# Where an expert's rows are zeroed and on which queue they are loaded: moving clears, loads and one weight split in a fused attention and mixture-of-experts kernel

## The chip, the cores and the metric

The kernel runs on one core of a Trainium2 chip. The metric is device time in microseconds (us), the median of several executions. One execution is recorded by the hardware profiler; its rows are what the prediction reads. PE is the matmul engine, PEld its weight loads, DVE the vector engine, ACT the scalar engine, POOL the GpSimd engine, SP the engine that only issues DMAs (its rows carry SPq).

## The reference, cut to what matters

Three layers follow each other; the output of one is the input of the next.

```python
# 1. recurrent attention over 2 x 8 heads, 768 positions, head size 48
for t in range(S):
    cur = einsum('bhd,bhe->bhde', u * k[t], v[t])
    y[t] = einsum('bhd,bhde->bhe', r[t], state + cur)
    state = w * state + einsum('bhd,bhe->bhde', k[t], v[t])
# 2. mixture of 8 experts, 1536 tokens of 384 numbers, each token to its best expert
expert = argmax(x @ w_gate); pos = rank of the token among those of its expert
disp[expert, pos] = x                      # dropped at capacity 384
y = relu(disp @ w1) @ w2                   # w1: 384 -> 1024, w2: 1024 -> 384
out = gate * y[expert, pos]                # 0 for a dropped token
# 3. gated MLP
out = (sigmoid(x @ w_gate2) * (x @ w_val)) @ w_out      # 384 -> 1536 -> 384
```

## The kernel before

**Stages.** Attention runs in eight steps `s` (a batch and a pair of heads each). The experts run in 64 steps `i` of one loop (line 1010), `i = 8e + f` for expert `e` and eighth `f` of its hidden layer. The gated MLP follows. The order of work on every engine is written out by hand: instructions go to each engine's queue in the order of the code, and each engine works through its own queue in that order.

**Rows of an expert.** Attention's output rows are sent to a table `xs_d` in device memory, 1536 rows for each expert, with indirect DMAs on POOL (`scatter`, line 231, twelve in all, six for each batch). A block of 224 rows per expert is read back. Rows of the block that no token fills must be zero. Before, this is done in two ways. For experts 0, 1 and 2 (`ZS = 3`), zeros are written to the whole block during attention step 3 from SP (line 742), where a source block `z_d` of zeros is written too. For experts 3 to 7, `clear(e)` (line 851) copies `z_d` over the 224 rows behind the expert's last token, at a place known only at run time, from POOL, at steps 11, 12, 13, 14 and 16 (`ZE`). Since the place is known only at run time, each of these copies counts as a write to the whole table: it waits for earlier copies and earlier reads of the table, and later reads wait for it.

**Loading an expert.** `eload(e)` (line 936) brings the 224 rows into a tile `xr` (two buffers). Expert 0 comes another way (`pre`, `first`). `eload(1)` is issued on POOL at step 0, `eload(2)` on SP at step 9, and `eload(e + 2)` on SP at `f == 7` of experts 1 to 5, so `eload(3)` at step 15 and `eload(4)` at step 23. `escale(e)` (line 943) then multiplies both halves by the gate on ACT, at step 7 for expert 1 and at `f == 3` of the expert before for the others (step 11 for expert 2, step 19 for expert 3). `etr(e, b)` (line 948) transposes half `b` on PE, and ACT and DVE split the result into a high and a low part; both halves share one buffer in PSUM. For expert 1 both are at step 8, each followed by an `s2`; for the others at `f == 4` and `f == 6` of the expert before.

**One step.** `s1` (nine matmuls, line 973) makes a piece of the hidden layer, ACT and DVE split it (lines 975, 976), and `s2` (six matmuls, lines 991 and 992) of a step three before adds to the output. `bg` (line 145) splits one raw weight tile of 128 x 768 into a high part on ACT (line 154) and a low part on DVE (line 156). Step `i` splits tile `n = 4 + i`, at the end of the step, behind that step's ACT work. Five raw buffers exist; `bg` of tile `n` first asks SP for tile `n + 5` (`fetch`, line 136), whose DMA waits until the buffer of tile `n` was read. `s1` of step `i` reads the tile with the largest even number not above `i`.

**Two extra waits.** Raw tile 5 waits for the landing of expert 0's rows, and raw tile 9 (`XG = 9`) for the landing of `eload(1)` (lines 142 and 143). Tile 9 is split at step 5.

**Decode.** From step 11 on, `tick` takes one piece at a time of the decode of the MLP's weights (lines 166 to 200), with a DMA of 768 KB for each tile on SP and a subtraction on POOL.

Of the kernel before, what the change touches and what calls it, by code (L numbers as in the profile page):

```python
# [21 lines left out]
AHEAD = 5  # L22
# [8 lines left out]
WE = 1  # L31
WF = 7
WG = 5
ZS = 3
ZE = {11: 3, 12: 4, 13: 5, 14: 6, 16: 7}
XG = 9
NKR = 3
NV = 4
ND = 5
# [1 line left out]
BG = (0, 0, 0, 0, 0, 0, 4, 0)  # L41
NB = 224
NP = NB // 2
# [5 lines left out]
MT = 5  # L49
HPB = 6  # L50
OVP = 60
BG2 = (56,)
NT = 2
TAILF = 4
EB0 = 8
# [61 lines left out]
def body(tc, A, out):  # L117
    nc = tc.nc
    E = mybir.EngineType
    with ExitStack() as top, tc.manual_schedule():  # L120
# [3 lines left out]
        xs_d = dr.tile([8 * 1536 + NB, XW], F32, tag="xs_d", name="xs_d")  # L124
        z_d = dr.tile([NB, XW], F32, tag="z_d", name="z_d")
# [10 lines left out]
        def fetch(n):  # L136
            while nxt[0] < n:
                m = nxt[0]
                nxt[0] += 1
                raw[m] = rpl[0].tile([128, 768], F32, tag="raw", name="raw", bufs=rpl[1])  # L140
                i = nc.sync.dma_start(out=raw[m], in_=A["wx"][m // 2][:, (m % 2) * 768:(m % 2) * 768 + 768])
                if m in (sum(BG) + 1, XG):
                    after(i, xr1l if m == XG else xr0l)

        def bg(count=1, pool=False, ahead=3, later=None, cast=nc.scalar.copy):
            for _ in range(count):
# [78 lines left out]
                    if k == 4:  # L225
                        last = n

        scx, sci, sco, xr0l, xr1l = [], [], [], [], []

        def scatter(done, group, dst, index, src, rows):  # L230
            i = nc.gpsimd.indirect_dma_start(  # L231
# [7 lines left out]
        def after(load, done):  # L239
            for i in done:  # L240
                tc.add_manual_dep(load.ins, i.name,
                                  mybir.DependencyInfo(mybir.DependencyClass.Sync, mybir.DependencyReason.DATA),
                                  reason="rows of every scatter")
# [22 lines left out]
        with ExitStack() as ctx:  # L266
# [17 lines left out]
            zero = cp.tile([128, 2, XW], F32, tag="zero", name="zero")  # L284
# [371 lines left out]
            def consts():  # L656
# [5 lines left out]
                nc.gpsimd.iota(tid, pattern=[[128, 12]], base=0, channel_multiplier=1)  # L662
                nc.gpsimd.tensor_copy(out=capf, in_=capi)

            def ok(q):
                return 0 <= q < 8

# [20 lines left out]
            for i in range(2):  # L688
# [7 lines left out]
                           in_=w128.unsqueeze(2).unsqueeze(2).to_broadcast([112, 4, 48, 4]))  # L696
# [34 lines left out]
            for s in range(8):  # L731
                nx, fu = s < 7, s < 6
                if s < 4:
                    load(s + 4, "k")
                if s < 5:
                    load(s + 3, "v")
                if s < 4:
                    load(s + 4, "d")
                fetch(sum(BG[:max(s + 2, 4)]) if s else 0)
                if s == 3:  # L740
                    for z in [xs_d[e * 1536:e * 1536 + NB, :] for e in range(ZS)] + [z_d]:
                        nc.sync.dma_start(out=z.rearrange("(p b) d -> p b d", b=2), in_=zero[0:NP])
                if s == 2:
                    consts()
                if nx:
                    ap0 = a_mm(s + 1, C0)
                    ap1 = a_mm(s + 1, C1)
                    u_pe(s + 1)
                subs = []
                y_own(s, C1)  # L750
                if s == 6:
                    diag(7, range(8, 12))
                out_evac(s, 1 if nx else 2)
                if nx:
                    out_tr(s)
                    a_cp(s + 1, C0, ap0)
                    u_scan(s + 1)
                    if s == 6:
                        bg(1, False, 0, subs, nc.vector.tensor_copy)
                        bg(BG[s] - 1, False, 0, subs)  # L760
                        subs.pop(0)()
                    out_x(s, s == 6)
                if s == 5:
                    r3b(0)
                    r3c(0)
                if fu:
                    rp(s + 2)
                    out_l(1)
                    sums(s + 2)
                    diag(s + 2, range(8))  # L770
                    out_l()
                    if s == 3:
                        r1a(0)
                    if s == 4:
                        r1o(0)
                    last = kb(s + 2)
                    a_cp(s + 1, C1, ap1)
                    if s < 5:
                        behind(kk_part(s + 2), last)
                        pr_part(s + 3, P_)  # L780
                    else:
                        kk_part(7, V_)
                if s == 6:
                    a_cp(7, C1, ap1)
                    for f in subs:
                        f()
                    cnt(0)
                if nx:
                    y_in(s + 1)
                    if s == 6:  # L790
                        y_own(7, (0, 1))
                        out_evac(7, 0)
                        y_own(7, (2, 3))
                        out_evac(7, 1)
                    else:
                        y_own(s + 1, C0)
                        out_evac(s + 1, 0)
                    if s < 5:
                        diag(s + 2, range(8, 12))
                    if s == 3:  # L800
                        r1m(0)
                    if s == 4:
                        r2(0)
                        r3a(0)
                        r1s(0)
            fetch(sum(BG) + 1)
            out_tr(7)
            warm_up(WF)
# [21 lines left out]
        with ExitStack() as ctx:  # L830
# [4 lines left out]
            xr, xt = {}, {}  # L835
# [15 lines left out]
            def clear(e):  # L851
                r = nc.values_load(zoi[0:1, e:e + 1], engines=[E.Pool], min_val=0, max_val=8 * 1536,
                                   skip_runtime_bounds_check_because="behind an expert's rows")
                nc.gpsimd.dma_start(out=xs_d[bass.ds(r, NB), :], in_=z_d)

            def overflow():
                with tc.If(offv["most"] > NB):  # L857
# [75 lines left out]
                offv[e] = nc.values_load(offi[0:1, e:e + 1], engines=[E.DVE, E.Activation], min_val=0, max_val=1536,  # L933
                                         skip_runtime_bounds_check_because="expert counts sum to the number of tokens")

            def eload(e, eng=nc.sync):
                xr[e] = mp.tile([128, 2, XW], F32, tag="xr", name="xr")
                i = eng.dma_start(out=xr[e][0:NP], in_=xs_d[e * 1536:e * 1536 + NB, :].rearrange("(b p) d -> p b d", p=NP))
                after(i, scx)
                if e == 1:  # L940
                    xr1l.append(i.ins)

            def escale(e):
                for b in range(2):
# [65 lines left out]
            for i in range(64 + LAG):  # L1010
                if i == OVP:
                    overflow()
                if i < 64:
                    e, f = seq[i]
                    if i == EB0:
                        for b in range(2):
                            etr(1, b)
                            s2(0, 5 + b)
                    s1(e, f)
                    if i == IC2:  # L1020
                        c2(0)
                        c2(1)
                    if i == IC1:
                        c1()
                    if i == OVL:
                        offv["most"] = nc.values_load(mxi[0:1, 0:1], min_val=0, max_val=1536,
                                                      skip_runtime_bounds_check_because="at most every token")
                    if i in ZE:
                        clear(ZE[i])
                    if f == 3 and e:  # L1030
                        c3(e)
                    if i == EB0 - 1 or f == EB[0] - 1 and 0 < e < 7:
                        escale(e + 1)
                    if f in EB and 0 < e < 7:
                        etr(e + 1, EB.index(f))
                    if f == 7 and 0 < e < 6 or i == 9:
                        eload(e + 2 if i != 9 else 2)
                if i >= LAG:
                    e, f = seq[i - LAG]
                    if i < 66 - TAILF:  # L1040
                        for g in (() if f == 0 and e else (0, 1) if f == 1 and e else S20.get(i, (f,))):
                            s2(e, g)
                        if (f == 7 if i > max(S20) else i == EB0):
                            for m in range(3):
                                yev(e, m)
                    elif i == 66:
                        for m in range(3):
                            for g in range(7 - TAILF, 8):
                                s2(7, g, (m,))
                            yev(7, m)  # L1050
                            xsplit(0, m)
                if i <= 58:
                    bg(2 if i in BG2 else 1, False, AHEAD)
                if i == 0:
                    eload(1, nc.gpsimd)
                if i == LOAD1:
                    tick()
                if i < 64:
                    tick(0 if i < T0 or OVP - NT <= i < OVP else TK if i < 51 else 2)
# [98 lines left out]
```

## Time and profile before

| | us |
|---|---|
| median of 3 executions | 457.27 |
| lowest, highest | 456.75, 458.99 |
| the profiled execution, its own time | 458.45 |
| its span, first to last instruction | 456.8 |
| PE busy in it | 435.9 (95%) |
| DVE busy | 283.4 (62%) |
| ACT busy | 226.1 (49%) |
| POOL busy | 108.4 (24%) |

Attention takes the first 76 us of the span, the experts run from 76 to 223 us, the gated MLP from 223 us to the end. Busy shares are averages over these three parts. In timelines a row is a start, a duration, an engine, a line and an operation, and in square brackets how long the engine had been idle before it and which instruction ended that. Rows of matmuls overlap in part, since matmuls are pipelined.

### The profile page before, as it was taken

What the parts mean: (1) busy time and instruction counts of PE and PEld (TensorE: products, weight loads), DVE (VectorE), ACT (ScalarE), POOL (GpSimd) and SP (SyncE); (2) the same over time, 40 slices, a digit from 0 to 9 for tenths busy, and PEclk for the clock granted to TensorE, in tenths of its full rate; (3) what the DMA queues carried; (4) which work ended last, traced back from release to release, by engine and by line L of the source; (5) the groups of instructions that cost most, each with busy time, mean ns of one, the idle gap of its engine ahead of it and who ended that gap; (6) DMA issues with size and microseconds to landing.
All of it is one profiled execution on the core that took longest, in us unless ns stands there. A gap on an engine that the chain in (4) does not pass through costs nothing.

```text
span 456.8 us, 8304 instructions
## 1 busy us (share of the span) xinstructions
PE 435.9 (95%) x3212; PEld 417.1 (91%) x3215; DVE 283.4 (62%) x498; ACT 226.1 (49%) x490; POOL 108.4 (24%) x107
## 2 busy tenths in 40 slices
PE   8999999899589999999999999999999999999993
PEld 4788888789589999999999999999999999999993
DVE  6888997559658898995577877778432221212211
ACT  5587687457357687775534353443442222222131
POOL 2466756000010110230033642322122000000013
PEclk9999999979869999999999999999999999999998
DMA  7999937558597987775025352431001000000002
GB/s 239 327 274 237 343 113 254 167 191 294 205 346 212 274 258 245 235 170 168 13 70 90 119 116 93 138 108 32 1 37 67 1 1 0 1 0 1 1 17 86
DMA packets 21946, 63.37 MB, mean 139 GB/s; under 512 B 4672, under 2 KB 6624, under 8 KB 21824
## 3 DMA queue, kind: packets, MB, share of 16 engines
q1 hardware_dynamic: 19584, 55.97, 40.9%
q0 software_dynamic: 2176, 6.84, 4.1%
q8 instruction: 26, 0.43, 0.4%
q14 instruction: 16, 0.13, 0.1%
q10 hardware_dynamic: 144, 0.00, 0.0%
HBM read 56.66 MB, written 7.88 MB: 141 GB/s over the span
## 4 chain that ended last, share of the span: by engine, by line
PE 51%; issue 1%; POOL 1%; POOLq 0%; ACT 0%
PE pg L1081 17%; PE pv L1081 16%; PE po L1106 16%; PE py L992 1%; PE ph L973 1%; POOL out_dram L231 1%; PE py L991 1%; POOLq L1154 0%; ACT sg L1087 0%; POOLq L231 0%
## 5 line engine op out<-in xcount | busy, mean ns | idle before, releaser
L1091 DVE TENSOR_TENSOR sg<-sg,pv 128x384 f32<-128x384 f32 (+2 forms) x49 | 26.6, 543 | 80.0 <-PE pv L1081 80.0
L156 DVE TENSOR_TENSOR rl<-raw,rh 128x768 fp32r<-128x768 f32 x60 | 59.9, 1000 | 20.0 <-ACT rh L154 19.6
L992 PE MATMUL py<-hh,rh 128*128 128x448 f32 x192 | 66.5, 387 | 0.0
L1092 ACT CAST gh<-sg 128x384 fp32r<-128x384 f32 (+2 forms) x49 | 24.8, 506 | 78.5 <-DVE sg L1091 78.4
L154 ACT CAST rh<-raw 128x768 fp32r<-128x768 f32 x63 | 52.2, 834 | 6.1 <-DMA raw<-in_wx_dram 5.7
L991 PE MATMUL py<-hh,rl 128*128 128x224 f32 x192 | 54.2, 282 | 0.0
L1093 DVE TENSOR_TENSOR gl<-sg,gh 128x384 fp32r<-128x384 f32 (+2 forms) x49 | 35.6, 727 | 28.9 <-ACT gh L1092 28.9
L1087 ACT ACTIVATE sg<-pg 128x384 f32<-128x384 f32 x48 | 23.6, 491 | 59.0 <-PE pg L1081 58.8
L200 POOL TENSOR_TENSOR wy<-wa,wy 128x768 fp32r<-128x768 f32 x10 | 19.7, 1968 | 107.9 <-ACT wy L196 107.9
L992 PEld LDWEIGHTS py<-hh,rh 128*128 128x128 f32 x192 | 38.0, 198 | 2.3
L975 ACT ACTIVATE hh<-ph 128x224 fp32r<-128x224 f32 x64 | 22.9, 357 | 34.8 <-PE ph L973 34.5
L231 POOL DMA_INDIRECT out_dram<-ob,ids x12 | 11.7, 974 | 118.5 <-ACT ob L1113 116.1
L991 PEld LDWEIGHTS py<-hh,rl 128*128 128x128 f32 x192 | 38.6, 201 | 0.0
L1106 PE MATMUL po<-wy,gh 128*128 128x384 f32 x144 | 36.6, 335 | 0.0
L976 DVE SCALAR_TENSOR_TENSOR hh<-ph,hh 128x224 fp32r<-128x224 f32 x64 | 24.6, 385 | 13.0 <-ACT hh L975 12.4
L419 ACT ACTIVATE at<-cst,dl 128x128 f32<-128x128 f32 x88 | 27.3, 389 | 5.8 <-DVE dl L405 4.8
L973 PE MATMUL ph<-xh,rh 128*128 128x224 f32 x96 | 26.6, 277 | 0.3 <-PEq L857 0.3
L973 PE MATMUL ph<-xl,rh 128*128 128x224 f32 x96 | 26.8, 279 | 0.0
L973 PE MATMUL ph<-xh,rl 128*128 128x224 f32 x96 | 26.7, 279 | 0.0
L973 PE MATMUL ph<-xeh,rh 128*128 128x224 f32 x96 | 26.6, 280 | 0.0
L973 PE MATMUL ph<-xel,rh 128*128 128x224 f32 x96 | 26.4, 279 | 0.0
L973 PE MATMUL ph<-xeh,rl 128*128 128x224 f32 x96 | 26.3, 278 | 0.0
(215 smaller groups left out, 1195.3 us busy)
## 6 DMA issues: line engine op xcount, KB each, us to landing
raw<-in_wx_dram SPq DMA_DIRECT2D x64, 384.0 KB, 4.8
r<-in_wy_dram SPq DMA_DIRECT2D x18, 768.0 KB, 5.5
kt<-in_kr_dram SPq DMA_DIRECT2D x7, 576.0 KB, 9.9
dm<-in_dm_dram SPq DMA_DIRECT2D x5, 672.0 KB, 12.4
v<-in_v_dram SPq DMA_DIRECT2D x8, 288.0 KB, 10.1
xr<-xs_d SPq DMA_DIRECT2D x6, 339.5 KB, 5.0
dm<-in_dm_dram SPq DMA_DIRECT2D x6, 288.0 KB, 11.8
xs_d<-z_d POOLq DMA_DIRECT2D x5, 339.5 KB, 5.5
```

The lines of the kernel that those rows point to most:

```text
L154: cast(out=h, in_=t)
L156: (nc.gpsimd if pool else nc.vector).tensor_sub(rl[n % NR], t, h.bitcast(F32))
L419: nc.scalar.mul(AT[s][:, j, :], ident, DL[s][:, j:j + 1])
L973: nc.tensor.matmul(ph, a[:, w], b[:, kt, :], start=(i == 0), stop=(i == 8))
L976: nc.vector.scalar_tensor_tensor(out=h[:, 1, :], in0=ph, scalar=0.0, in1=h[:, 0, :].bitcast(F32), op0=ALU.max, op1=ALU.subtract)
L991: nc.tensor.matmul(y[:, 0, :], wl[:, w], h[:, 0, :], start=(f == 0), stop=False, skip_group_check=True)
L992: nc.tensor.matmul(y, wh[:, w], h, start=False, stop=(f == 7), skip_group_check=True)
L1081: nc.tensor.matmul(pg[g], w[a][:, q], x[b][:, kt, :], start=(kt == 0 and (a, b) == (0, 0)), stop=(kt == 2 and b == 1))
L1091: nc.vector.tensor_mul(gg[:, a:b], sg[:, a:b], pg[1][:, a:b])
L1092: nc.scalar.copy(out=gh[:, a:b], in_=gg[:, a:b])
L1093: nc.vector.tensor_sub(gl[:, a:b], gg[:, a:b], gh[:, a:b].bitcast(F32))
L1106: nc.tensor.matmul(po[i], g[v][:, a], w[u][:, q], start=(f == 0 and (u, v) == (0, 0)), stop=(f == 11 and v == 1))
```

## The change

- `ZS` goes from 3 to 5: the blocks of experts 0 to 4 are zeroed during attention step 3, and the source block `z_d` is written at step 6 in place of step 3.
- The clears that are left, for experts 5, 6 and 7, move to steps 21, 22 and 23, and are declared independent of one another.
- `eload(1)` moves from POOL's queue to SP's, at the same step 0, which is ahead of raw tile 9 in SP's queue. Raw tile 9 no longer waits for its landing.
- `eload(e + 2)` of experts 1 to 5 moves from `f == 7` to `f == 4`: `eload(3)` from step 15 to 12, `eload(4)` from 23 to 20, `eload(5)` from 31 to 28.
- Step 5 splits no weight tile, and step 11 splits two. From step 6 to step 10, a step splits tile `3 + i`.

```diff
-ZS = 3
-ZE = {11: 3, 12: 4, 13: 5, 14: 6, 16: 7}
-XG = 9
+ZS = 5
+ZE = {21: 5, 22: 6, 23: 7}
+GE = 4
-BG2 = (56,)
+BG2 = (11, 56)
+BG0 = (5,)
...
-                if m in (sum(BG) + 1, XG):
-                    after(i, xr1l if m == XG else xr0l)
+                if m == sum(BG) + 1:
+                    after(i, xr0l)
...
+            def zfill(d):
+                nc.sync.dma_start(out=d.rearrange("(p b) d -> p b d", b=2), in_=zero[0:NP])
...
                 if s == 3:
-                    for z in [xs_d[e * 1536:e * 1536 + NB, :] for e in range(ZS)] + [z_d]:
-                        nc.sync.dma_start(out=z.rearrange("(p b) d -> p b d", b=2), in_=zero[0:NP])
+                    for e in range(ZS):
+                        zfill(xs_d[e * 1536:e * 1536 + NB, :])
+                if s == 6:
+                    zfill(z_d)
...
-                nc.gpsimd.dma_start(out=xs_d[bass.ds(r, NB), :], in_=z_d)
+                i = nc.gpsimd.dma_start(out=xs_d[bass.ds(r, NB), :], in_=z_d).ins
+                tc.declare_no_dep(i, group="zc", reason="each expert has rows of its own")
+                tc.add_to_no_dep_group("zc", i)
...
-            def eload(e, eng=nc.sync):
+            def eload(e):
                 xr[e] = mp.tile([128, 2, XW], F32, tag="xr", name="xr")
-                i = eng.dma_start(out=xr[e][0:NP], in_=xs_d[e * 1536:e * 1536 + NB, :].rearrange("(b p) d -> p b d", p=NP))
-                after(i, scx)
-                if e == 1:
-                    xr1l.append(i.ins)
+                after(nc.sync.dma_start(out=xr[e][0:NP], in_=xs_d[e * 1536:e * 1536 + NB, :].rearrange("(b p) d -> p b d", p=NP)), scx)
...
-                    if f == 7 and 0 < e < 6 or i == 9:
+                    if f == GE and 0 < e < 6 or i == 9:
                         eload(e + 2 if i != 9 else 2)
...
-                    bg(2 if i in BG2 else 1, False, AHEAD)
+                    bg(0 if i in BG0 else 2 if i in BG2 else 1, False, AHEAD)
                 if i == 0:
-                    eload(1, nc.gpsimd)
+                    eload(1)
```

## Rows read from the trace of the kernel before

**Rows 1.** The page: TensorE's granted clock, tenths, in 40 equal slices.

```profile
PEclk9999999979869999999999999999999999999998
```

**Rows 2.** Waits of PE: who waited, for whom; us in total, times, longest us.

```profile
PE xp L955 <- ACT xr L946: 8.9, 3, 6.2
...
PE ap L438 <- DVE dm L397: 0.9, 2, 0.6
PE xp L955 <- DVE xl L959: 0.5, 1, 0.5
```

**Rows 3.** Timeline of PE, 85 to 100 us, steps 6 to 9.

```profile
85.38 0.27 PE L973 MATMUL ph<-xeh,rh 128*128 128x224 f32 x1
...
87.33 0.27 PE L973 MATMUL ph<-xeh,rh 128*128 128x224 f32 x1
...
89.07 0.37 PE L992 MATMUL py<-hh,rh 128*128 128x448 f32 x1
91.78 0.51 PE L955 MATMUL xp<-cst,xr 112*128 112x112 f32 x3 [2.34 <-ACT xr L946]
...
94.41 0.82 PE L955 MATMUL xp<-cst,xr 112*128 112x112 f32 x3 [0.53 <-DVE xl L959]
...
99.90 0.26 PE L973 MATMUL ph<-xh,rh 128*128 128x224 f32 x1
```

**Rows 4.** Timeline of ACT, 84 to 93 us.

```profile
84.64 0.36 ACT L975 ACTIVATE hh<-ph 128x224 fp32r<-128x224 f32 x1 [0.85 <-PE ph L973]
89.04 0.83 ACT L154 CAST rh<-raw 128x768 fp32r<-128x768 f32 x1 [4.04 <-DMA raw<-in_wx_dram]
...
91.12 1.11 ACT L946 ACTIVATE xr<-xr 112x384 f32<-112x384 f32 x2
92.13 0.82 ACT L154 CAST rh<-raw 128x768 fp32r<-128x768 f32 x1
```

**Rows 5.** Timeline of POOL, 78 to 121 us.

```profile
78.54 0.98 POOL L231 DMA_INDIRECT xs_d<-xs,pi  x1 [0.31 <-issue]
82.31 0.76 POOL L938 DMA_DIRECT2D xr<-xs_d  x1 [2.79 <-DVE rl L156]
...
110.53 0.49 POOL L854 DMA_DIRECT2D xs_d<-z_d  x1 [5.23 <-DMA xs_d<-z_d]
...
120.06 0.49 POOL L854 DMA_DIRECT2D xs_d<-z_d  x1 [2.92 <-DMA xs_d<-z_d]
```

**Rows 6.** Waits of SP, columns as in rows 2.

```profile
SPq L141 <- DMA xr<-xs_d: 13.5, 1, 13.5
...
SPq L938 <- DMA xs_d<-z_d: 12.1, 1, 12.1
```

**Rows 7.** Timeline of SP, 85 to 124 us.

```profile
85.95 1.75 SPq L141 DMA_DIRECT2D raw<-in_wx_dram  x4
...
123.12 0.33 SPq L938 DMA_DIRECT2D xr<-xs_d  x1
```

**Rows 8.** Timeline of PE, 104 to 134 us, steps 12 to 21.

```profile
104.48 0.51 PE L955 MATMUL xp<-cst,xr 112*128 112x112 f32 x3 [0.27 <-ACT xr L946]
...
106.73 0.27 PE L973 MATMUL ph<-xh,rh 128*128 128x224 f32 x1
...
127.11 0.82 PE L955 MATMUL xp<-cst,xr 112*128 112x112 f32 x3 [6.25 <-ACT xr L946]
...
133.17 0.36 PE L991 MATMUL py<-hh,rl 128*128 128x224 f32 x1
```

**Rows 9.** Line 938: its DMAs on SP and POOL, us to landing.

```profile
DMA to landing us min/median/max: 3.3/4.9/7.5
```

**Rows 10.** Windows: length, busy us (instructions) by engine, granted clock, DMA share, GB/s.

```profile
50.00:55.00 5.00, 5.00 (x85) 4.39 (x84) 4.72 (x12) 4.47 (x14) 3.69 (x3) 1.00 1.04 396
95.00:100.00 5.00, 5.00 (x25) 4.83 (x23) 1.05 (x3) 1.33 (x4) 0.00 (x0) 0.58 0.56 173
...
180.00:190.00 10.00, 10.00 (x77) 9.74 (x77) 10.00 (x16) 8.00 (x15) 2.34 (x1) 1.00 0.69 189
```

More of the change, by code (lines that the diff above doesn't have):

```diff
@@ L226, in tick @@
                         last = n
-        scx, sci, sco, xr0l, xr1l = [], [], [], [], []
+        scx, sci, sco, xr0l = [], [], [], []
         def scatter(done, group, dst, index, src, rows):
```

## The prediction, made before the changed kernel was run

> **What bounds the kernel now.** I read PE's row of the page first: 95% busy, so it looks as if nothing but fewer matmuls could help. The slices of granted clock say otherwise: 9 nearly everywhere, but 7, 9, 8, 6 in slices 9 to 12, which are 91 to 137 us, inside the expert stage [rows 1]. Next the waits of PE: the largest entry by far is the transpose of an expert's rows waiting for ACT's scaling, 8.9 us in three pieces, one of 6.2 [rows 2]. PE's timeline puts them in place. At step 8 PE idles 2.34 us, then 0.53 us [rows 3]; at step 20 it idles 6.25 us [rows 8]. Behind both, matmuls run at the lower of the clock's two levels: a transpose group that takes 0.51 us takes 0.82, and the window from 95 to 100 us has a granted clock of 0.58 [rows 3, 8, 10]. "Busy" hides that half.
>
> What each costs. At full speed a step of one s1 and one s2 is 87.33 − 85.38 = 1.95 us [rows 3], and the block of one transposition and two s2 is 106.73 − 104.48 = 2.25 us [rows 8]; so an s2 or an s1 is about 0.97 and a transposition 0.3. First place: PE ran dry at 91.78 − 2.34 = 89.44 and came out at full speed at 99.90, 10.46 us, for two transpositions, three s2 and one s1: 2.25 + 0.3 + 1.95 = 4.5. Lost: **6.0 us**. Second place: dry at 127.11 − 6.25 = 120.86, at full speed from 133.17: 12.3 us for 2.25 + 0.97 = 3.2. Lost: **9.1 us**.
>
> Then back from each stall. First: ACT scales expert 1's rows at 91.12. It comes late because ACT stood 4.04 us at raw tile 9, until 89.04 [rows 4]. Raw tile 9 was late because SP held it for the landing of eload(1), 13.5 us of waiting [rows 6], and let it go at 85.95 [rows 7]; eload(1) itself was issued on POOL at 82.31, when the scatters (the last at 78.54) had landed [rows 5]. Second: eload(3) left SP only at 123.12 [rows 7], after 12.1 us behind the clears [rows 6], and the clears stood in a chain: each waits for the one before, 5.23 + 0.49 = 5.7 us apiece [rows 5]. A landing of 3.3 us [rows 9] gives 126.4; ACT scales, PE goes on at 127.11.
>
> **Part by part, second place first.** eload(3) now stands at step 12 and no clear is ahead of it in any queue. Its buffer, last read at step 8, is free. ACT needs it at step 19, seven steps or 13.7 us later; behind it on SP only raw tiles and decode loads queue, and a landing of at most 7.5 us [rows 9] leaves 6 us. The stall goes whole: −9.1 us. What is late next there is the order on ACT itself, as at step 12 in the trace, where the transposition waited 0.27 us [rows 8]; I add 0.
>
> The three clears that are left cost POOL 0.49 us each [rows 5]. They now wait for eload(4)'s reading, which puts them at about step 22.5. Queued behind them on POOL is one decode subtraction, whose result ACT needs only when its buffer comes round again, two tiles of decode (over ten steps) later. eload(5), on SP at step 28, waits for them: 5.5 steps, 10.7 us, after they start. Bounds: independent, they land together some 5.7 us after the start (cover 5 us); in a chain, 17.1 us, which is a rival. In bytes, steps 20 to 25 ask for five raw tiles, eload(4), one decode load and three clears, about 4.2 MB, 10.5 us at the 396 GB/s of a window with full DMA share [rows 10], in five steps of 1.95 = 9.75 us: under 1 us late, and a raw tile is asked for five steps (9.7 us) ahead while raw tile 9 took 89.04 − 85.95 = 3.1 us [rows 4, 7]. I add 0; without that cover it would be the 0.8 us. The earlier loads 4 to 7 take three steps more of lead, worth nothing once they are on time; each finds its buffer read four steps or more before.
>
> **First place.** SP now holds eload(1) until the scatters have landed. That is not in the trace for SP; POOL's start at 82.31 is the late end, the issue of the last scatter, 79.5, the early end. I take 82.3. With a landing of 4.9 us (3.3 to 7.5) the rows are there at 87.2 (85.6 to 89.8). Raw tile 9 goes right behind, at about 82.7 instead of 85.95, and by its 3.1 us is there at 85.8. ACT: step 5 ends without a split, after the hidden piece at 84.64; the next follow at 86.6 and 88.5, one step apart [rows 4]. Tile 9 is split between these two, from 86.95 on, on time. At 88.85 ACT scales; the first half is done 0.66 us later (91.78 − 91.12), 89.5, just when PE arrives (89.44). So the 2.34 us go.
>
> But the second half of the transposition waits for the buffer of the first, and DVE's share of that waits behind the split of a raw tile. In the trace the second transposition began 94.41 − 91.12 = 3.29 us after the scaling began, with a tile split in between [rows 3, 4]. The change keeps that order at step 7 and 8. 88.85 + 3.29 = 92.1; PE has done one transposition and one s2 by 89.44 + 0.3 + 0.97 = 90.7. So a new gap of **1.4 us** takes the place of 2.34 + 0.53. Everything then hangs on the clock: it held through a wait of 0.6 us in attention [rows 1, 2] and fell at the 2.34 us. 1.4 is a little nearer to 0.6 (0.8 away) than to 2.34 (0.9), and I take it that it holds: −6.0 + 1.4 = −4.6 us. If it falls, the low level costs about half of the stretch it lasts: 133.17 − 127.11 = 6.1 us, so 3.0 us [rows 8].
>
> The Trainium skill speaks against the move to SP: in "DMA: Bandwidth & Descriptors", section "Issuing engines are not separate DMA queues", it says that transfers from all issuing engines run on the same 16 DMA engines and interleave, and that another issuer saves only the issue time. Rows 5 bear out the second half (0.76 us on POOL); by the first half eload(1) would share with raw tiles 9 to 12 and land at the late end, 89.8, which adds about 1 us to the gap. The sum would be −3.6 us, or −0.6 with the clock.
>
> **Small edits.** Attention writes five blocks of zeros and, later, z_d, six transfers for four. Bounds: nothing, or two transfers of 339.5 KB at 396 GB/s, 1.8 us, if attention waits for its loads, since the DMA share is full there [rows 10]. No entry of PE's waits names a DMA; the longest for work on loaded data is 0.9 us in two pieces, for DVE's scaling of `dm` [rows 2]. I take 0. The pause moves one split (0.83 ACT [rows 4]) from step 5 to step 11: tiles 9 to 13 come a step later, three steps ahead of their matmuls in place of four; nothing waits. At step 11 it puts 0.83 us on ACT and the low part on DVE, behind the scaling of expert 2 and so not ahead of what PE awaits at step 12; the result of step 12's hidden piece is used three steps later. 0, or 0.8 without that cover. From there on DVE is near its own bound (10.00 of 10 us from 180 on, beside PE's 10.00 [rows 10]), but PE does not wait for it.
>
> **Sum.** −9.1 − 4.6 = −13.7 us. The profiled execution took 458.45, 1.2 above the median of 457.27 and inside the spread of the three; its span would go from 456.8 to 443.1. The median: 457.27 − 13.7 = **443.6 us**.
>
> **Rivals.**
> - The clock falls at the new gap of 1.4 us. For it: nothing in the trace between 0.6 and 2.34; a late eload(1) lengthens the gap. Against: PE works at full clock right before and after. 443.6 + 3.0 = 446.6; with the late load 447.6. Chance 0.22.
> - The change doesn't do all it says: the clears stay in a chain. They end 17.1 us after step 22.5, 6.4 us past step 28; SP stands, and raw tiles with it, against a cover of 9.7 − 3.1 = 6.6 us. 0 to 1.5 us of idle PE, 443.6 to 445, or 448 if the clock falls too. Chance 0.08.
> - The first stall stays, since raw tile 9 or the rows still reach ACT late behind four other transfers. Only the second place pays: 457.3 − 9.1 = 448.2. Chance 0.05.
> - Slower than before: the stall of step 20 comes back at step 28, larger. Place: eload(5) on SP behind the clears, and every raw tile behind it. It eats the whole gain when PE idles 10.7 us and pays 3.0 for the clock: SP would stand 10.7 + 6.6 = 17.3 us past step 28, so the three clears would take 10.7 + 17.3 = 28 us, 9.3 us each in a chain, against 5.7 [rows 5]. From there each us more is a us over 457.3; at 11 us apiece it is 462. Chance 0.03.
> - Within 0.5% of before, by a mixture of these: 0.02.
>
> **How the numbers follow.** The forecast has 0.60: 443.6, its own range 442.2 (no new gap at all) to 445.2 (the small covers gone, 0.8 + 0.8). The range runs from 442.2 up to the first rival with half of its late load, 447.4; the rest of the rivals above that and the tails hold under 2 in 10. Faster by over 0.5% (2.3 us, about what a measurement of this kernel can tell from no change): 0.95; within: 0.02; slower: 0.03.
>
> **What would show it.** In the changed profile: SP's wait of raw tile 9 for eload(1) and that of line 938 for the clears are gone; ACT has no wait for a raw tile near 86; PE's waits for ACT's scaling fall from 8.9 us to under 1; a wait of the transposition for DVE of about 1.4 us stands near 91; the clock's slices 9 to 12 read 9. A clock under 1 near 92 to 99 is the first rival; a wait of SP for the clears after step 28 the second or the fourth. I am wrong if the gated MLP, from 210 us on, does not simply start 13.7 us earlier.

## The result, and the profile after

The changed kernel takes **445.75 us** (445.32 to 446.98) against 457.24 us for the kernel before: a ratio of 0.9746, 95% interval 0.9714 to 0.9778, or 11.5 us less. 443.6 was forecast, with a range of 442.2 to 447.4: right in direction and range, but the gain is 2.2 us short of the 13.7 us of the sum. 445.75 also lies above the forecast's own range of 442.2 to 445.2; it is inside the wide one because that was stretched for a falling clock, which did not come. The profiled execution took 445.70 us, with a span of 444.1, against 458.45 and 456.8: in that pair the gain is 12.7 us. Both shortfalls, 1.0 in the profiles and 1.2 more in the medians, have a cause of their own below.

The page of the changed kernel, granted clock, and the waits of its PE (columns as in rows 2; the last line is again in the list):

```profile
PEclk9999999999999999999999999999999999999998
```

```profile
PE xp L960 <- DVE xl L964: 1.2, 1, 1.2
PE ph L978 <- DVE rl L157: 0.9, 1, 0.9
PE ap L439 <- DVE dm L398: 0.9, 2, 0.6
```

The dips of the clock in rows 1 are gone. The 8.9 us of waiting for ACT's scaling in rows 2 have left the list; the transposition's wait for DVE has grown from 0.5 to 1.2 us, and one of 0.9 us for the low part of a weight tile is new. The timeline of PE shows where they lie; lines have moved by five, so 973 is now 978 and 955 is 960:

```profile
89.21 0.37 PE L997 MATMUL py<-hh,rh 128*128 128x448 f32 x1
...
92.22 0.51 PE L960 MATMUL xp<-cst,xr 112*128 112x112 f32 x3 [1.17 <-DVE xl L964]
...
95.74 0.27 PE L978 MATMUL ph<-xh,rh 128*128 128x224 f32 x1
...
99.00 0.28 PE L978 MATMUL ph<-xl,rh 128*128 128x224 f32 x1
100.23 0.37 PE L978 MATMUL ph<-xh,rl 128*128 128x224 f32 x1 [0.95 <-DVE rl L157]
...
210.59 0.51 PE L1086 MATMUL pg<-x0h,wy 128*128 128x384 f32 x2
```

The stretch that began at 89.44 and ended at 99.90 in rows 3 now runs from 89.58 (89.21 + 0.37) to 95.74: 6.2 us in place of 10.5. In place of rows 8 there is no wait between 101 and 211 us but one of 0.30 us at 198.97, which the kernel before has too (0.30 at 211.47). The gated MLP starts at 210.59. In the kernel before it started at

```profile
223.09 0.51 PE L1081 MATMUL pg<-x0h,wy 128*128 128x384 f32 x2
```

which is 12.5 us later, all of it won between 76 us and there. From the first matmul of line 978 (76.29) to the first of line 1086 the expert stage takes 134.3 us; before, it took 146.95. Below, "expert stage" means this stretch, read in the same way.

ACT and DVE around step 8, in the timeline after:

```profile
84.78 0.36 ACT L980 ACTIVATE hh<-ph 128x224 fp32r<-128x224 f32 x1 [0.87 <-PE ph L978]
86.72 0.36 ACT L980 ACTIVATE hh<-ph 128x224 fp32r<-128x224 f32 x1 [1.59 <-PE ph L978]
86.98 0.83 ACT L155 CAST rh<-raw 128x768 fp32r<-128x768 f32 x1
88.67 0.36 ACT L980 ACTIVATE hh<-ph 128x224 fp32r<-128x224 f32 x1 [0.86 <-PE ph L978]
88.92 1.11 ACT L951 ACTIVATE xr<-xr 112x384 f32<-112x384 f32 x2
```

```profile
90.79 0.96 DVE L157 TENSOR_TENSOR rl<-raw,rh 128x768 fp32r<-128x768 f32 x1 [1.34 <-ACT rh L155]
91.67 0.50 DVE L964 TENSOR_TENSOR xl<-xp,xh 128x336 fp32r<-128x336 f32 x1
...
95.85 0.98 DVE L1002 TENSOR_TENSOR x<-x,py 128x224 f32<-128x224 f32 x3
97.06 0.96 DVE L157 TENSOR_TENSOR rl<-raw,rh 128x768 fp32r<-128x768 f32 x1 [0.22 <-ACT rh L155]
...
98.23 0.16 DVE L847 COPY cf<-ct 128x8 f32<-128x8 f32 x1
...
99.24 0.94 DVE L157 TENSOR_TENSOR rl<-raw,rh 128x768 fp32r<-128x768 f32 x1
```

ACT's stand of 4.04 us in rows 4 is gone; the scaling starts at 88.92 (88.85 was worked out). The low part of a raw tile (90.79) stands ahead of the low part of expert 1's first half (91.67), which releases the second transposition at 92.22. The row at 99.24 is the low part of raw tile 12, which step 12 awaits until 100.23; ahead of it on DVE stand expert 0's output (95.85), the low part of tile 11 (97.06) and the counts of tokens (from 98.23).

SP and POOL after:

```profile
80.91 0.35 SPq L946 DMA_DIRECT2D xr<-xs_d  x1
...
104.28 0.43 SPq L946 DMA_DIRECT2D xr<-xs_d  x1
```

```profile
124.54 0.58 POOL L860 DMA_DIRECT2D xs_d<-z_d  x1 [45.56 <-DMA raw<-in_wx_dram]
125.47 0.51 POOL L860 DMA_DIRECT2D xs_d<-z_d  x1 [0.34 <-issue]
126.00 1.88 POOL L201 TENSOR_TENSOR wy<-wa,wy 128x768 fp32r<-128x768 f32 x1
127.78 0.52 POOL L860 DMA_DIRECT2D xs_d<-z_d  x1
```

Expert 1's rows leave SP at 80.91 (82.3 was taken), expert 3's at 104.28 in place of 123.12 [rows 7]. The three clears start within 3.3 us, none behind another's landing as in rows 5.

### The profile page after: what moved, and what is told of

It is laid out like the page before. It is cut to its first block, busy times and chain, and to the rows that moved or that the text cites. A ratio compares the mean times of both kernels' runs of the same rounds, so it can differ in the third digit from the quotient of the medians.

```text
span 444.1 us, 8306 instructions
## 1 busy us (share of the span) xinstructions
PE 430.4 (97%) x3212; PEld 411.7 (93%) x3215; DVE 283.7 (64%) x498; ACT 225.5 (51%) x490; POOL 105.5 (24%) x104
## 4 chain that ended last, share of the span: by engine, by line
PE 52%; issue 1%; POOL 1%; POOLq 0%; ACT 0%
PE pg L1086 17%; PE pv L1086 16%; PE po L1111 16%; PE py L997 1%; PE ph L978 1%; POOL out_dram L232 1%; PE py L996 1%; POOLq L1159 0%; ACT sg L1092 0%; POOLq L232 0%
## 5 line engine op out<-in xcount | busy, mean ns | idle before, releaser
L157 DVE TENSOR_TENSOR rl<-raw,rh 128x768 fp32r<-128x768 f32 x60 | 61.1, 1021 | 9.1 <-ACT rh L155 8.8
L997 PE MATMUL py<-hh,rh 128*128 128x448 f32 x192 | 63.4, 372 | 0.0
L996 PE MATMUL py<-hh,rl 128*128 128x224 f32 x192 | 52.5, 273 | 0.0
L997 PEld LDWEIGHTS py<-hh,rh 128*128 128x128 f32 x192 | 36.3, 189 | 2.0
L996 PEld LDWEIGHTS py<-hh,rl 128*128 128x128 f32 x192 | 36.7, 191 | 0.0
L981 DVE SCALAR_TENSOR_TENSOR hh<-ph,hh 128x224 fp32r<-128x224 f32 x64 | 24.7, 386 | 11.5 <-ACT hh L980 11.3
L1111 PEld LDWEIGHTS po<-wy,gh 128*128 128x128 f32 x144 | 26.0, 188 | 0.0
## 6 DMA issues: line engine op xcount, KB each, us to landing
dm<-in_dm_dram SPq DMA_DIRECT2D x5, 672.0 KB, 12.5
```

The lines of the kernel that those rows point to most:

```text
L157: (nc.gpsimd if pool else nc.vector).tensor_sub(rl[n % NR], t, h.bitcast(F32))
L981: nc.vector.scalar_tensor_tensor(out=h[:, 1, :], in0=ph, scalar=0.0, in1=h[:, 0, :].bitcast(F32), op0=ALU.max, op1=ALU.subtract)
L996: nc.tensor.matmul(y[:, 0, :], wl[:, w], h[:, 0, :], start=(f == 0), stop=False, skip_group_check=True)
L997: nc.tensor.matmul(y, wh[:, w], h, start=False, stop=(f == 7), skip_group_check=True)
L1111: nc.tensor.matmul(po[i], g[v][:, a], w[u][:, q], start=(f == 0 and (u, v) == (0, 0)), stop=(f == 11 and v == 1))
```

## The experiments

Theory: the sum is right part by part for the execution it was read from; the shortfall is the split pause, priced at 0, and an execution of the kernel before that was slower than the median. Rivals: the pause is needed; the second place gave less; the two places depend on each other; the queue, not the wait, made the first gain; the declared independence of the clears made the second.

The runs were timed on three chips, A, B and C, each time beside the kernel before, which took 457.12, 462.76 and 457.43 us there. Ratios are taken within a chip; of these only chip C timed the changed kernel too, so on A and B a difference from its 445.75 us is not one side by side.

| kernel | chip | us | ratio to before (95%) | expert stage, us |
|---|---|---|---|---|
| before, first profile | - | 457.24 | 1 | 146.95 |
| changed, first profile | - | 445.75 | 0.9746 (0.9714 to 0.9778) | 134.30 |
| e1_no_pause | A | 444.83 | 0.9721 (0.9683 to 0.9758) | 133.59 |
| e2_first_only | A | 455.16 | 0.9953 (0.9926 to 0.9980) | 143.33 |
| e3_second_only | A | 448.62 | 0.9791 (0.9738 to 0.9843) | 137.78 |
| e4_pair6 | A | 444.85 | 0.9722 (0.9684 to 0.9760) | 133.69 |
| e5_pool_load | B | 454.98 | 0.9806 (0.9763 to 0.9849) | 134.76 |
| e6_chain | B | 455.68 | 0.9827 (0.9778 to 0.9876) | 135.99 |
| e7_pair7 | B | 454.70 | 0.9825 (0.9783 to 0.9867) | 136.04 |
| e9_split_after_pair | B | 451.25 | 0.9749 (0.9715 to 0.9784) | 132.71 |
| a1_changed_again | C | 446.31 | 0.9746 (0.9716 to 0.9776) | 136.06 |
| e10_split_after_pair | C | 443.99 | 0.9705 (0.9674 to 0.9736) | 132.65 |
| e8_late_loads | C | 446.63 | 0.9777 (0.9732 to 0.9822) | 134.34 |
| b1_before_again | C | 457.31 | - | 145.57 |

On chip B PE also stood in attention, near 60 to 66 us, in waits that the profile puts down to no one ("issue"), and the clock fell there in the profiles of e5, e6 and e7; for the kernels on that chip the expert stage, which begins later, is the better measure, and their whole times say little to a microsecond. The stage has a spread of its own: two profiles of the changed kernel gave 134.30 and 136.06 us, two of the kernel before 146.95 and 145.57. A smaller difference between two single profiles shows nothing by itself; there the waits named in the rows carry the reading.

**The pause alone undone.**

```
-BG2 = (11, 56)
-BG0 = (5,)
+BG2 = (56,)
+BG0 = ()
```

> The changed kernel without the pause: step 5 splits raw tile 9 again, step 11 one tile. Theory: in the changed kernel tile 9 is in its buffer near 85 us, about when step 5 comes to it, so the pause protects nothing; what it does is to put tiles 9 to 13 a step later, and the low part of tile 12 then comes 0.95 us too late for step 12, where PE runs four hidden pieces with no output piece between. Without the pause that wait of 0.95 us for DVE goes and the wait of about 1.2 us for the transposed rows stays: 445.75 - 0.95 = 444.8. Rival: the pause is what keeps ACT from standing at tile 9; without it ACT waits again near 86 us, expert 1's rows are scaled late, PE idles 2 us or more at step 8 and the clock falls: 448 or more.

444.83 us and a ratio of 0.9721. It was not timed beside the changed kernel, and the intervals of the two ratios overlap; the profile is plainer. ACT waited for raw tile 9 for 0.71 us at step 5, and PE never felt it. The wait at step 12 is gone, and a small one for the scaling of expert 2 took a part of its place:

```profile
91.77 0.51 PE L960 MATMUL xp<-cst,xr 112*128 112x112 f32 x3 [1.17 <-DVE xl L964]
...
99.87 0.51 PE L960 MATMUL xp<-cst,xr 112*128 112x112 f32 x3 [0.27 <-ACT xr L951]
```

0.95 us less 0.27 us is 0.68; the expert stage is 0.71 shorter. In these profiles the pause protects nothing that PE waits for and costs 0.7 us.

**The first place alone.**

```
-                    eload(1, nc.gpsimd)
+                    eload(1)
...
-                if m in (sum(BG) + 1, XG):
-                    after(i, xr1l if m == XG else xr0l)
+                if m == sum(BG) + 1:
+                    after(i, xr0l)
```

and the pause, put into the kernel before.

> The kernel before with the first place alone changed: expert 1's rows loaded on SyncE ahead of raw tile 9, which no longer waits for their landing, and the pause. Theory: the stall of step 8 shrinks from 6.0 us lost to about 1.7, the new wait of 0.95 us at step 12 comes, the stall of step 20 stays with its 9.1 us: 457.24 - 3.4 = 453.8. Rival (the two places are not independent; a run that is early reaches the chain of clears earlier and waits there longer): the clears stand where they stood, so the gain is eaten at step 20 and the time is 456 to 457.2.

455.16 us, 2.0 less than before, where 3.4 was expected. Against the first profile the expert stage is 3.6 us shorter (146.95 − 143.33), close to the 3.4; against the second profile of the kernel before, 2.2, which is what the medians say. The rival is partly true too: PE came to step 20 earlier and waited there 0.5 us longer than the 6.25 of rows 8.

```profile
123.92 0.82 PE L955 MATMUL xp<-cst,xr 112*128 112x112 f32 x3 [6.75 <-ACT xr L946]
...
128.87 0.27 PE L973 MATMUL ph<-xel,rh 128*128 128x224 f32 x1
```

**The second place alone**, the changed kernel with the lines of the first place put back and without the pause.

```
+XG = 9
...
-                    eload(1)
+                    eload(1, nc.gpsimd)
```

> The changed kernel with the first place undone: expert 1's rows on GpSimdE, raw tile 9 waiting for their landing, no pause; zeros, clears and the places of the loads as in the changed kernel. Theory: only the stall of step 20 is gone, 9.1 us: 457.24 - 9.1 = 448.1, with the wait of 2.3 us and the low clock near 92 us as in the kernel before. Rival (the change came out 2 us short since the second place gave less): 450 or more.

448.62 us, 8.5 less than before; 9.1 was expected, and in the profiles the expert stage is 9.2 us shorter than in the first profile of the kernel before (146.95 − 137.78) and 7.8 than in the second. The profiled execution was the longest of the four (450.58 us): the clock also fell in attention, from 12.0 to 18.6 us, and the stage began 1.4 us late (77.61). No wait is left at step 20. The first place is as it was: a gap of 2.17 us, one of 0.66, and behind that a transposition at the lower clock (0.82 us).

```profile
93.07 0.51 PE L964 MATMUL xp<-cst,xr 112*128 112x112 f32 x3 [2.17 <-ACT xr L955]
...
95.71 0.82 PE L964 MATMUL xp<-cst,xr 112*128 112x112 f32 x3 [0.66 <-DVE xl L968]
```

**The pair earlier and the pause later.**

```
-BG2 = (11, 56)
-BG0 = (5,)
+BG2 = (6, 56)
+BG0 = (7,)
```

> The changed kernel with the pause at step 7 in place of step 5, and the two tiles at step 6 in place of step 11. Theory: at step 7 no low part of a raw tile stands on DVE ahead of the low part of expert 1's first half, so the wait of 1.2 us for it goes; tiles 9 to 12 are as early as without any pause, so the wait of 0.95 us at step 12 goes too: 445.75 - 2.1 = 443.6. Rival: both waits are the pace of ACT and DVE after step 8 and only move (to step 9 or step 12): 445 to 446.

444.85 us, 0.9 below the changed kernel's 445.75 (not timed side by side; the expert stage is 0.6 us shorter) and 1.3 above what the theory gave. The wait at step 12 went, as expected, and so did the wait for DVE between the two transpositions. But two splits at step 6 ask for raw tile 11 before it has landed. ACT stood at it and the scaling came a microsecond later, so the same 1.17 us stand ahead of the first transposition:

```profile
89.02 0.83 ACT L155 CAST rh<-raw 128x768 fp32r<-128x768 f32 x1 [1.29 <-DMA raw<-in_wx_dram]
...
90.00 1.11 ACT L951 ACTIVATE xr<-xr 112x384 f32<-112x384 f32 x2
```

```profile
90.66 0.51 PE L960 MATMUL xp<-cst,xr 112*128 112x112 f32 x3 [1.17 <-ACT xr L951]
```

Neither the theory nor its rival had this; it is the stall of the kernel before on a small scale.

**The queue of expert 1's rows.**

```
-                    eload(1)
+                    eload(1, nc.gpsimd)
```

in the changed kernel; raw tile 9 still waits for nothing.

> The changed kernel with expert 1's rows loaded from GpSimdE again, raw tile 9 still waiting for nothing. Theory: what paid at step 8 was that raw tile 9 no longer waits, not the queue that carries the rows; the rows land by 87 us, before ACT asks for them at 88.9: 445.75, no change. Rival (the section of the Trainium skill's page on DMA that says transfers of all issuing engines interleave on the same 16 engines): raw tiles 9 to 12 now leave before the rows and share the engines with them, the rows land at 89.8 or later, the wait of PE at step 8 grows by 1 us or more and the clock may fall: 446.7 to 449.7.

The expert stage takes 134.76 us against 134.30, and the two gaps are those of the changed kernel, 1.18 and 0.95. Raw tile 9 left SP at 90.43, two microseconds ahead of the rows on POOL (92.53), and ACT scaled them at 99.30 without a wait:

```profile
92.53 0.77 POOL L946 DMA_DIRECT2D xr<-xs_d  x1 [3.17 <-ACT rh L155]
```

```profile
99.30 1.11 ACT L951 ACTIVATE xr<-xr 112x384 f32<-112x384 f32 x2
```

```profile
102.61 0.51 PE L960 MATMUL xp<-cst,xr 112*128 112x112 f32 x3 [1.18 <-DVE xl L964]
```

The 0.46 us are within the spread between executions (a wait of 0.36 at 128 us is most of them). The whole time, 0.9806 of before on chip B, does not tell theory from rival; the profile does: with the rows on POOL and no wait on raw tile 9, ACT's stand and the falling clock at step 8 stay away. So the first gain came from the wait that was taken off raw tile 9, not from the queue. The Trainium skill ("DMA: Bandwidth & Descriptors", section "Issuing engines are not separate DMA queues") says that another issuing engine saves only the issue time; this run agrees. That the transfers then slow each other enough to matter here, which I had drawn from it, does not show: this trace has no landing for the load on POOL itself, but ACT scaled its rows 6.8 us after the issue without waiting, and the six loads on SP landed within 5.9 us.

**The clears in a chain again.**

```
-                i = nc.gpsimd.dma_start(out=xs_d[bass.ds(r, NB), :], in_=z_d).ins
-                tc.declare_no_dep(i, group="zc", reason="each expert has rows of its own")
-                tc.add_to_no_dep_group("zc", i)
+                nc.gpsimd.dma_start(out=xs_d[bass.ds(r, NB), :], in_=z_d)
```

> The changed kernel with the three clears in a chain again (each waits for the one before). Theory: they end some 17 us after they start near 124.5 us, the load of expert 5 leaves SyncE some 4 to 6 us late with the raw tiles behind it, and the five raw tiles ahead cover that: 445.75 to 446.5. Rival (the declared independence carries the gain of the second place): PE runs dry after step 30 and the clock falls: 449 or more.

The expert stage is 1.7 us longer than in the changed kernel's first profile (135.99). The chain is back, 134.46, 140.61 and 146.06 on POOL; SP stood 5.1 us at expert 5's rows, ACT then waited twice for raw tiles (1.1 and 1.8 us), and PE once, near step 36:

```profile
SPq L944 <- DMA xs_d<-z_d: 5.1, 1, 5.1
```

```profile
161.09 0.51 PE L958 MATMUL xp<-cst,xr 112*128 112x112 f32 x3 [0.99 <-ACT xr L949]
```

The clock held in the expert stage. The 0.99 us lie inside the 0 to 1.5 us that the prediction gave this case, and a little above what the theory of the run allowed; the other 0.7 us I did not place; they are within the spread of the stage. In this profile the independence of the clears is worth about a microsecond, not the 9: those come from taking clears out of the way of expert 3's rows. Whether fewer clears or later ones did it was not run apart.

**A wider gap at step 8.**

```
-BG2 = (11, 56)
+BG2 = (7, 56)
```

> The changed kernel with the two tiles at step 7 in place of step 11, to widen the gap at step 8 from 1.2 us to 2.1 us (one more low part on DVE ahead of the transposed rows'), between the 1.2 us at which the clock held and the 2.3 us at which it fell. The wait of 0.95 us at step 12 goes, since tile 12 is split at step 8 again. Theory: the clock still falls only at more; the two changes cancel: 445.75. Rival: at 2.1 us the clock falls, for 2.4 to 3 us more: 448.2 to 448.8.

The gap is 2.04 us, the clock fell, and came back 3.2 us after the gap ended. The wait at step 12 went; the expert stage is 1.7 us longer than in the changed kernel's first profile.

```profile
99.49 0.82 PE L960 MATMUL xp<-cst,xr 112*128 112x112 f32 x3 [2.04 <-DVE xl L964]
...
102.72 0.31 PE L978 MATMUL ph<-xl,rh 128*128 128x224 f32 x1
102.87 0.28 PE L978 MATMUL ph<-xh,rl 128*128 128x224 f32 x1
```

The rival holds in kind; in size the fall cost half of 3.2 us, 1.6, less than the 2.4 to 3 I had given it. The parts, 0.9 more gap, 0.95 less at step 12 and 1.6 for the clock, make 1.55.

**The raw tile of step 7 behind the transpositions.**

```
-BG2 = (11, 56)
-BG0 = (5,)
+BG2 = (56,)
+BG0 = (7,)
...
                             etr(1, b)
                             s2(0, 5 + b)
+                        bg(1, False, AHEAD)
```

> No pause at step 5 and no pair at step 11; the tile of step 7 is split inside step 8, behind both transpositions of expert 1's rows. Theory: the wait of 1.2 us at step 8 is the low part of that raw tile standing on DVE, and its high part on ACT, ahead of the parts of the transposed rows; behind them the tile costs nothing, since it comes back before step 10. Against the kernel without the pause (444.83 us): 444.83 - 1.2 = 443.7. Rival: ACT and DVE are behind at step 8 whatever the order, the wait moves to the output rows of expert 0 or to step 12: 444.8.

> The kernel whose tile of step 7 is split behind both transpositions of expert 1's rows, beside the changed kernel on one chip. Its expert stage was 132.7 us against 134.3 of the changed kernel. Theory: that is worth 1.6 to 2.1 us of the whole time, here too. Rival: the shorter stage only meets other waits, and the two are within 0.5 us.

On chip B its time stands at 0.9749 of before, which tells little there; its expert stage of 132.71 us is 1.6 shorter than the changed kernel's and 0.9 shorter than without the pause. On chip C it took 443.99 us against the changed kernel's 446.31 on the same chip: 2.3 us less, and 0.9705 of the kernel before. Its stage there, 132.65 us, agrees with the first. Both gaps are gone; the one wait left between 76 and 140 us is

```profile
98.73 0.51 PE L960 MATMUL xp<-cst,xr 112*128 112x112 f32 x3 [0.27 <-ACT xr L951]
```

This version beats both kernels. The wait of 1.2 us was the order on ACT and DVE, as said, and nothing took its place.

**The changed kernel again.**

> The changed kernel once more, beside the others of this call. Theory: it stands to the kernel before as it did, 0.9746 of its time; its expert stage takes 134.3 us and has the two waits of 1.2 and 0.95 us.

The ratio is the same to four digits. The profiled execution was the longest of its six (447.36 us), and its expert stage is 1.8 us longer than in the first profile: besides the two known waits it has one of 0.44 us and this one, after ACT had waited 1.8 us for a decode load and 3.1 us in three pieces for raw tiles:

```profile
111.48 0.90 ACT L177 ACTIVATE wa<-r 128x768 f32<-128x768 f32 x1 [1.80 <-DMA r<-in_wy_dram]
```

```profile
135.62 0.51 PE L960 MATMUL xp<-cst,xr 112*128 112x112 f32 x3 [1.21 <-ACT xr L951]
```

**The loads at the last step of an expert again.**

```
-GE = 4
+GE = 7
```

> The changed kernel with the loads of experts 3 to 7 back at the last step of an expert (steps 15, 23, 31, 39, 47); clears and zeros as in the changed kernel. Theory: the second place was paid by the clears that no longer stand ahead of expert 3's rows, and the earlier loads pay nothing: the same time as the changed kernel in this call, within 0.5 us. Rival: the clears at steps 21 to 23 now stand ahead of expert 4's rows (step 23), which ACT scales at step 27, so a small wait of PE, up to 2 us, comes at step 28.

446.63 us beside 446.31, and 134.34 us beside 134.30 in the first profile: the earlier loads pay nothing. SP did stand 5.7 us behind a clear, and PE has no wait from it.

```profile
SPq L946 <- DMA xs_d<-z_d: 5.7, 1, 5.7
```

**The kernel before again.**

> The kernel before, unchanged, for a second profile. Theory: the idle gaps near 90 and 121 us are those of the first profile (2.3 and 6.3 us), but the time for which the clock stays at its lower level behind each differs from execution to execution by up to some 3 us, which is the spread of the times of this kernel. Rival: both falls last as long as in the first profile (6.8 and 6.1 us of low clock while matmuls run), and the spread comes from elsewhere.

457.31 us, within 0.1 of the median on its chip. Its gaps at step 8 are 1.52 and 1.77 us in place of 2.34 and 0.53, the clock fell only in the second of them, and both stretches of low clock end sooner: the clock is back at 97.7 and at 131.9 us, and was back at 99.2 and 133.3 in the first profile.

```profile
91.17 0.51 PE L955 MATMUL xp<-cst,xr 112*128 112x112 f32 x3 [1.52 <-ACT xr L946]
...
94.42 0.82 PE L955 MATMUL xp<-cst,xr 112*128 112x112 f32 x3 [1.77 <-DVE xl L959]
...
99.21 0.27 PE L973 MATMUL ph<-xh,rh 128*128 128x224 f32 x1
```

```profile
126.19 0.82 PE L955 MATMUL xp<-cst,xr 112*128 112x112 f32 x3 [6.01 <-ACT xr L946]
...
132.07 0.28 PE L991 MATMUL py<-hh,rl 128*128 128x224 f32 x1
```

Worked as in the prediction: dry from 91.17 − 1.52 = 89.65 to 99.21, 9.6 us for 4.5 of work, 5.1 lost; dry from 120.18 to 132.07, 11.9 for 3.2, 8.7 lost. That is 13.8 us against the 15.1 of the first profile.

## Why the prediction was right, and where it fell short

- **Second place, −9.1 us: right.** From step 12 to the end of the expert stage the changed kernel is 9.1 us shorter than the first profile of before (104.48 to 223.09 against 101.11 to 210.59). Alone (e3) it gave 8.5 us in the medians, and 9.2 or 7.8 in the profiles. The earlier loads were rightly priced at 0 (e8).
- **The clears at steps 21 to 23, 0: right.** Independent, they delay nothing; in a chain they cost PE 0.99 us, inside the 0 to 1.5 us given.
- **First place, −4.6 us: right in mechanism, 0.3 us too much.** ACT does not stand at raw tile 9, the scaling starts at 88.92, and a new gap stands where it was said, with the cause that was said: 1.17 us, 1.4 forecast. The clock held. But the stretch at step 8 shrank by 10.46 − 6.16 = 4.3 us: the work in it, counted as 4.5 us, took 5.0 (6.16 − 1.17) in the changed profile. That a gap of 2.0 us would have made it fall is shown by e7; the first rival was near. That the clock would hold rested on 1.4 lying a little nearer to 0.6 than to 2.34, with nothing in the trace between them: a guess that came out.
- **"Tiles 9 to 13 come a step later, three steps ahead of their matmuls in place of four; nothing waits": this step failed.** I counted the lead in steps of 1.95 us. From step 9 to 12 PE runs four hidden pieces back to back, with no output piece between, so the three steps are some 3 us. DVE, behind it with expert 0's output and the counts (from line 847 on, 842 in the kernel before), finished tile 12's low part at 100.2, and PE waited 0.95 us. The term is 0.7 to 0.95 us, not 0, near the 0.8 that the prediction named as the price without cover. With the 0.3 us above it is most of what the prediction's own sign missed by: the gated MLP starts 12.5 us earlier, not 13.7.
- **The subtraction from the median failed by 1.2 us.** 13.7 us was worked out from an execution of 458.45 us. Against its own time the sum gives 444.75, and with the pause's 0.95, 445.7: the profiled execution of the changed kernel took 445.70. That this meets to the hundredth is chance: term by term the expert stage gave 4.3 − 0.8 + 9.1 = 12.6 us. Against the median, the losses of an execution that lies at the median are to be used: 13.8 − 1.2 − 0.95 = 11.6, and 11.5 was measured. The prediction saw the 1.2 us and called them spread. In the two profiles of the kernel before they are the length of the low clock behind the two stalls (the idle gaps themselves add up to 9.1 and 9.3 us), and the change removes it.
- **Crowded DMA, 0 for under 1 us: right in the execution at the median.** A longer one shows it: 1.65 us of waiting PE in a1, behind late loads.
- **More zeros in attention, 0: right.** The expert stage starts at 76.29 us, at 76.14 in the first profile of before and at 76.37 in the second.

## What to carry to other kernels

Price a lost lead in the time of the steps that follow it, not in a mean step: the same lead of three steps was 6 us in most of the stage and 3 us where one kind of matmul ran alone. Work out stalls from a profile that lies at the median, or subtract from the profiled execution and not from the median, above all where the clock falls behind the stall. And when two small pieces share a buffer, put nothing of the background between them on the engines that hand it over: moving one split behind them took a wait of 1.2 us away and made the stage 0.9 us shorter.

## What the runs showed of the hardware

The clock held through single gaps of 1.17 to 1.21 us in each profile that has one and through one of 1.52 us; it fell in a gap of 1.77 us that began 1.5 us after that one had ended, and in or just behind gaps of 2.04, 2.17 and 2.34 us. The length of one gap does not decide it alone. In attention on chip B the clock fell among gaps of at most 1.12 us that followed each other within some 6 us (e5, e6, e7), and held where they were at most 0.82 (e9). In e3 and e5 it fell near 12 us behind gaps of at most 0.76 us. In the long gap at step 20 it stayed at the upper level for 2.2 us in the first profile of before, and for 4.8 and 4.9 us in e2 and in the second.

Matmuls then ran at half rate (granted clock 0.50, the 1.2 GHz level) for 3.2 and 3.3 us (e7, and step 8 of the second profile of before), 4.9 us (e2), 5.7 and 6.2 us (step 20 of before) or 6.8 us (step 8 of the first profile of before, and e3). The spread of the kernel before goes with this: on chip A its shortest execution, 454.83 us, had a mean granted clock of 0.989, its longest, 460.53, one of 0.971; the kernel without the pause, at 0.995 to 0.998, stayed between 444.52 and 445.15. A spread alone is no sign of a falling clock: e8, in whose profile it does not fall, went from 445.56 to 449.17 us at 0.993 to 0.996.
